# A table of powers on one partition, heads innermost, read in pieces of 4 KB

## The chip, the cores and the metric

The program runs on one core of a Trainium2 chip. What is measured is the time of one execution on the device, in microseconds (us). The core has a matrix engine (PE, TensorE), a vector engine (DVE), a scalar engine (ACT), a general engine (POOL), a queue engine that issues most transfers (SP), and 16 DMA engines that move data between HBM and the on-chip memory (SBUF). Matrix products are written to PSUM.

## The reference

Attention with a decay per head, block by block, followed by two gated layers. Cut to what matters here:

```
pos = arange(64);  rel = pos[:, None] - pos[None, :]
Dmask     = where(rel >= 0, lam ** rel, 0)            # per head, 8 heads
lam_pow   = lam ** (pos + 1);  lam_block = lam ** 64
rev_pow   = lam ** (63 - pos)
for each block b of 64 rows:
    intra = (q_b k_b^T * Dmask) v_b
    inter = (q_b * lam_pow) kv_state
    out_b = intra + inter
    kv_state = lam_block * kv_state + (k_b * rev_pow)^T v_b
x = out as (1536 tokens, 512)
h = x w_in;  g = h * tanh(softplus(h));  x = g w_out
h = x w2_in; g = max(h, 0)^2;            result = g w2_out
```

`q`, `k`, `v` are (2, 8, 768, 64), `lam` has 8 values between 0.97 and 0.99, `w_in` and `w2_in` are (512, 2048), `w_out` and `w2_out` (2048, 512). All is fp32.

## The kernel before

The kernel takes chunks of 128 rows in place of the blocks of 64: twelve chunks, six for each of the two batches, taken in pairs by `attention(j)`. The eight heads are four pairs (index `p` or `n`) times two (index `e`). For every chunk it loads `qk` and `kv` (512 KB each), makes the scores `sc` on PE (L392), multiplies them by the mask into `a` on DVE (the operation of L395, recorded as L271), weights `k` by the mask's last column on POOL (`kd`, L398) and `q` by the decays on POOL (`qd`, L403, not for the first chunk of a batch), makes the state's increment `sd` on PE (L415), scales the state by lam to the 128 (L451 on ACT in the first pairs, L447 on POOL later) and adds the increment on DVE (tile `state`). The output `xo` sums products of `a` with `v` (L433) and of the weighted `q` with the state (L437). It is split into a high and a low part (`xh` on ACT, `xl` on DVE) for the layers, whose products are `up`, `p`, `b`, `e` and `dn` (all recorded as L278). The weights arrive as 64-bit numbers in tiles `st`, from which `m` (ACT, L507), `t` (DVE, L510 and L515), `wh` (ACT) and `wl` (DVE) are made.

The mask and the decays come from one table of powers of `lam`. It lies on eight partitions, one for each head, as 256 columns: 127 zeros, a one, and lam to the 1 to 128 (`tab`, L300). `lam` is loaded into it by a transfer from ACT's queue (L334), `ones` writes the zeros and the one (L331, L332), `powers` doubles the number of filled columns seven times (L324). The table is written to HBM (`tab_d`, L338) and then read back so that partition j gets the table shifted by j: for the mask two transfers (L344), one for each `e`, whose innermost runs are 128 elements of one head (512 bytes), and for the decays two more (L351), the same runs repeated over 64 partitions each. In SBUF the mask is laid out as (e, pair, column), like the scores.

All operations are given to a planner with an estimated duration each. It fills the engines by due times and writes down one order, and every engine works through its instructions in that order. `FIRST` (L241) fixes the order of the first transfers on SP's queue: st00000, qk0, tab_d, kv0, st00001, masks, decays, qk1, kv1, qk2, kv2, qk3, kv3. Every instruction waits for the data it needs, and those behind it on its engine wait with it. On-chip tiles of 4 KB per partition are handed out by the planner (`UNITS` of them) and given back after the last use. A number behind a name counts chunks (`a0` is the first `a`, `qk5` the sixth `qk`).

Of the kernel before, what the change touches and what calls it, by code (L numbers as in the profile page):

```python
# [12 lines left out]
F32 = mybir.dt.float32  # L13
# [7 lines left out]
P = 128  # L21
# [195 lines left out]
def attention_mlps(ctx, tc, lam, qk, kv, w_in, w_out, w2_in, w2_out, out):  # L217
# [52 lines left out]
    def tt(o, a, b, alu):  # L270
        nc.vector.tensor_tensor(out=o, in0=a, in1=b, op=alu)  # L271
# [19 lines left out]

    W = 2 * CH
    tab_d = dram.tile([H, W], F32, name="tab_d")
    misc = Val("misc")
    mask = Val("mask")

    def pw():
        return tl(misc, 2, 4, CH)[:, 0]

    def tab():  # L300
        return tl(misc, 4, W)[0:H, 2]

# [8 lines left out]
    misc_parts = [(misc, "pw"), (misc, "tab")]  # L311
# [9 lines left out]
    def powers():  # L321
        t, o, n = tab(), CH - 1, 1
        while n < CH:
            nc.vector.tensor_scalar(  # L324
                out=t[:, o + n + 1 : o + 2 * n + 1], in0=t[:, o + 1 : o + n + 1],
                scalar1=t[:, o + n : o + n + 1], scalar2=None, op0=ALU.mult,
            )
            n *= 2

    def ones():  # L330
        nc.vector.memset(tab()[:, 0 : CH - 1], 0.0)  # L331
        nc.vector.memset(tab()[:, CH - 1 : CH], 1.0)  # L332

    op("ACT", 0.1, lambda: nc.scalar.dma_start(out=tab()[:, CH : CH + 1], in_=lam), [], [(misc, "lam")],  # L334
       name="lam", lag=2.2, due=0.0)
    op("DVE", 0.4, ones, [], [(misc, "tab")], name="ones")
    op("DVE", 1.2, powers, [(misc, "lam")], [(misc, "tab")], name="powers")
    op("SP", 0.1, lambda: nc.sync.dma_start(out=tab_d, in_=tab()), [(misc, "tab")], [("tab_d", 0)],  # L338
       name="tab_d", lag=2.2, due=FIRST["tab_d"])

    def masks():
        for e in range(2):

            nc.sync.dma_start(  # L344
                out=tl(mask, 2, NP, CH)[:, e],
                in_=bass.AP(tab_d.tensor, tab_d.offset + e * W, [[1, P], [2 * W, NP], [1, CH]]),
            )

    def decays():
        for e in range(2):  # L350
            nc.sync.dma_start(  # L351
                out=pw()[e * D : (e + 1) * D],
                in_=bass.AP(tab_d.tensor, tab_d.offset + e * W + CH, [[0, D], [2 * W, NP], [1, CH]]),
            )

    op("SP", 1.6, masks, [("tab_d", 0)], [(mask, 0)], name="masks", due=FIRST["masks"])
# [526 lines left out]
```

## Time and profile before

| what | us |
|---|---|
| median of 3 runs | 566.46 (566.30 to 566.48) |
| the profiled execution | 566.5 |
| its span, from first to last instruction | 564.7 |
| PE busy | 549.6 (97%) |
| PEld (weight loads, beside PE) busy | 454.9 |
| ACT busy | 333.2 |
| DVE busy | 307.6 |
| POOL busy | 33.1 |

The page gives the busy time of each engine, the span in 40 slices, and the chain of work that ended last. A timeline lists instructions in order of time: start, duration (of all merged instructions together), engine, line, operation, output<-inputs, shapes, count, and in brackets how long the engine had been idle before and what ended that. An engine's name with a small q (SPq) is its queue, where transfers are issued. All times count from the span's start.

### The profile page before, as it was taken

Reading aid. Unit: us, or ns where it says so; the run is one execution under the profiler, and the core shown is the slowest. Engines: PE = TensorE matmul, PEld = TensorE weight load, DVE = VectorE, ACT = ScalarE, POOL = GpSimd, SP = SyncE. Lnnn points to the kernel's source line nnn. Section 1 sums busy time; section 2 is a strip of 40 time slices with the busy share of each in tenths; the row PEclk is TensorE's granted clock in tenths of the full one; section 3 lists DMA queues with packets and bytes.
Section 4 is the critical chain, followed back from the end, with each engine's and each line's share of the span. In section 5 each row is a group of like instructions: output and inputs, shape, how many; then the busy total and the mean of one; then the engine's idle time right before and its main releaser. Section 6 shows DMA issues by size and latency. Waiting matters only on the chain.

```text
span 564.7 us, 7047 instructions
## 1 busy us (share of the span) xinstructions
PE 549.6 (97%) x2934; PEld 454.9 (81%) x2934; DVE 307.6 (54%) x339; ACT 333.2 (59%) x374; POOL 33.1 (6%) x31
## 2 busy tenths in 40 slices
PE   3989999999999999999999999999999999999997
PEld 1878888888888888888888888888888888888885
DVE  2876985951453833582688865434363635743301
ACT  1435364643764566545886877347964789546920
POOL 1654600000000000000000000000000000000000
PEclk9899999999999999999999999999999999999999
DMA  8999000222141106041400401311222112300022
GB/s 238 409 409 339 6 2 0 75 74 74 38 149 38 38 2 203 21 122 65 149 1 0 150 0 38 111 39 37 76 74 75 60 48 79 113 0 1 18 95 111
DMA packets 15998, 50.52 MB, mean 89 GB/s; under 512 B 1624, under 2 KB 3168, under 8 KB 15968
## 3 DMA queue, kind: packets, MB, share of 16 engines
q1 hardware_dynamic: 15952, 50.08, 25.5%
q8 instruction: 23, 0.38, 0.3%
q14 instruction: 7, 0.06, 0.0%
q10 hardware_dynamic: 16, 0.00, 0.0%
HBM read 46.92 MB, written 3.15 MB: 89 GB/s over the span
## 4 chain that ended last, share of the span: by engine, by line
PE 96%; DMA 2%; DVE 1%; issue 0%; SPq 0%; DVEq 0%
PE dn L278 46%; PE up L278 20%; PE p L278 13%; PE e L278 7%; PE b L278 3%; PE xo L433 2%; PE sc L392 2%; PE xo L437 1%; DMA mask<-tab_d 1%; PE sd L415 1%; DVE t L510 0%; DMA tab_d<-misc 0%; DVE state L271 0%; DVE misc L324 0%; DMA misc<-in_lam_dram 0%
## 5 line engine op out<-in xcount | busy, mean ns | idle before, releaser
L515 DVE SCALAR_TENSOR_TENSOR t<-m,t 128x1024 int32<-128x1024 int32 x64 | 78.5, 1231 | 63.5 <-ACT m L507 61.4
L268 ACT ACTIVATE ac<-dn 128x1024 f32<-128x1024 f32 x46 | 47.3, 1029 | 101.9 <-PE dn L278 101.9
L271 DVE TENSOR_TENSOR gl<-h,gh 128x1024 fp32r<-128x1024 f32 x48 | 58.7, 1227 | 78.0 <-ACT gh L268 77.6
L278 PE MATMUL dn<-gh,wl 128*128 128x512 f32 x192 | 74.7, 389 | 0.0
L278 PE MATMUL dn<-wh,gh 128*128 128x512 f32 x192 | 74.7, 389 | 0.0
L278 PE MATMUL dn<-wh,gl 128*128 128x512 f32 x192 | 74.7, 389 | 0.0
L278 PE MATMUL dn<-gh,wh 128*128 128x512 f32 x192 | 74.7, 389 | 0.0
L278 PE MATMUL dn<-wl,gh 128*128 128x512 f32 x192 | 74.7, 389 | 0.0
L278 PE MATMUL dn<-gl,wh 128*128 128x512 f32 x192 | 74.7, 389 | 0.0
L268 ACT ACTIVATE gh<-h 128x1024 fp32r<-128x1024 f32 x48 | 50.3, 1053 | 0.7
L507 ACT ACTIVATE m<-st 128x512 f32<-128x512 f32 x64 | 40.1, 664 | 10.5 <-DMA st<-in_moe_w_in_dram 6.8
L271 DVE TENSOR_TENSOR wl<-t,wh 128x1024 fp32r<-128x1024 f32 x32 | 39.6, 1246 | 12.1 <-ACT wh L268 12.1
L606 ACT ACTIVATE h<-up 128x1024 f32<-128x1024 f32 x20 | 20.6, 1029 | 38.2 <-PE up L278 32.5
L268 ACT ACTIVATE wh<-t 128x1024 fp32r<-128x1024 f32 x32 | 33.4, 1052 | 15.3 <-DVE t L515 15.2
L278 PEld LDWEIGHTS dn<-gh,wl 128*128 128x128 f32 x192 | 36.0, 188 | 7.5
L278 PEld LDWEIGHTS dn<-wh,gh 128*128 128x128 f32 x192 | 36.0, 188 | 7.5
L278 PEld LDWEIGHTS dn<-gl,wh 128*128 128x128 f32 x192 | 36.0, 188 | 7.5
L278 PEld LDWEIGHTS dn<-wl,gh 128*128 128x128 f32 x192 | 36.0, 188 | 7.5
L278 PEld LDWEIGHTS dn<-wh,gl 128*128 128x128 f32 x192 | 36.0, 188 | 7.4
L278 PEld LDWEIGHTS dn<-gh,wh 128*128 128x128 f32 x192 | 36.0, 188 | 7.4
L268 ACT ACTIVATE dn<-ac 128x1024 f32<-128x1024 f32 x34 | 34.4, 1019 | 0.2
L510 DVE TENSOR_SCALAR t<-st 128x512 int32<-128x512 int32 x64 | 26.8, 446 | 7.0 <-DMA st<-in_moe_w_in_dram 5.7
(102 smaller groups left out, 987.3 us busy)
## 6 DMA issues: line engine op xcount, KB each, us to landing
st<-in_moe_w_in_dram SPq DMA_DIRECT2D x32, 512.0 KB, 4.7
st<-in_moe_w_out_dram SPq DMA_DIRECT2D x32, 512.0 KB, 3.6
qk<-in_qk_dram SPq DMA_DIRECT2D x12, 512.0 KB, 10.6
kv<-in_kv_dram SPq DMA_DIRECT2D x12, 512.0 KB, 10.4
out_dram<-ac SPq DMA_DIRECT2D x4, 512.0 KB, 2.8
out_dram<-ac SPq DMA_DIRECT2D x4, 256.0 KB, 2.0
mask<-tab_d SPq DMA_DIRECT2D x2, 256.0 KB, 6.3
misc<-tab_d SPq DMA_DIRECT2D x2, 128.0 KB, 6.8
```

What stands on the lines that cost most here:

```text
L268: nc.scalar.activation(out=o, in_=i, func=AF.Copy)
L271: nc.vector.tensor_tensor(out=o, in0=a, in1=b, op=alu)
L278: nc.tensor.matmul(out=out_, lhsT=a, rhs=b, start=first and i == 0 and not onto, stop=last and i == 2, skip_group_check=onto)
L392: nc.tensor.matmul(out=o[:, e, p], lhsT=t[r, 1, p], rhs=t[r, 0, p], start=True, stop=True)
L415: nc.tensor.matmul(out=o[e * D : (e + 1) * D, p], lhsT=t[:, p, 1 + e], rhs=t[:, p, 0 if e else 3], start=True, stop=True)
L433: nc.tensor.matmul(out=o[e * D : (e + 1) * D, p, n], lhsT=v[:, p, 0 if e else 3], rhs=w[:, e, p], start=True, stop=fresh)
L437: nc.tensor.matmul(out=o[r, p, n], lhsT=z[:, p, r], rhs=qd[:, p], start=False, stop=True)
L507: op("ACT", 0.67, lambda st=st, i=i: nc.scalar.activation(out=tl(m)[:, i], in_=tl(st, TB, 2)[:, :, 1].bitcast(F32), func=AF.Copy, scale=RA ...
L510: op("DVE", 0.5, lambda st=st, i=i: nc.vector.tensor_scalar(out=tl(t)[:, i], in0=tl(st, TB, 2)[:, :, 0], scalar1=29, scalar2=None, op0=ALU ...
L515: nc.vector.scalar_tensor_tensor(out=tl(t), in0=tl(m).bitcast(I32), scalar=scalar, in1=tl(t), op0=shift, op1=ALU.bitwise_or)
L606: op("ACT", 1.05, lambda: nc.scalar.activation(out=tl(h), in_=tl(src), func=AF.Relu if L else AF.Mish), halves(src), [(h, 0)], name=h.name)
```

## The change

The table now lies on one partition in two tiles of 4 KB, with the eight heads innermost: element (column, head). `ones` and `powers` work on whole rows of eight heads, `powers` with a product of two operands, the second repeated. `lam` is loaded as one row of eight. The table is written to HBM by two transfers, one for each tile. The mask is read by one transfer whose rows are 4 KB long, each starting eight elements after the one before; the decays by two transfers whose rows are 4 KB less one element. In SBUF mask and decays keep the order (column, head), so `a` (through `weighting`) and `qd` (through `pw`) read them with a step of eight elements. The planner's estimates for `powers`, `masks` and `decays` change from 1.2, 1.6 and 0.9 to 2.0, 0.8 and 0.6 us.

```diff
     W = 2 * CH
-    tab_d = dram.tile([H, W], F32, name="tab_d")
+    tab_d = dram.tile([1, W * H], F32, name="tab_d")
     misc = Val("misc")
+    table = [Val("tab0"), Val("tab1")]
     mask = Val("mask")
     def pw():
-        return tl(misc, 2, 4, CH)[:, 0]
-    def tab():
-        return tl(misc, 4, W)[0:H, 2]
+        return tl(misc, CH, NP, 2)[:, :, :, 0].rearrange("p i n -> p n i")
+    def weighting():
+        return tl(mask, CH, NP, 2).rearrange("p i n e -> p e n i")
+    def tab(lo, hi):
+        t, b = table[lo // CH], lo // CH * CH
+        return tl(t, CH, H)[0:1, lo - b : hi - b]
     def warm_up():
@@ -308,7 +315,6 @@
     warm = Val("warm", "P")
     zval = Val("zero", dtype=BF16)
-    misc_parts = [(misc, "pw"), (misc, "tab")]
     def zeros():
         if zval.tile is None:
@@ -319,42 +325,46 @@
     op("PE", 4.3, warm_up, [(zval, 0)], [(warm, 0)], name="warm", rank=-3000)
     def powers():
-        t, o, n = tab(), CH - 1, 1
+        o, n = CH - 1, 1
         while n < CH:
-            nc.vector.tensor_scalar(
-                out=t[:, o + n + 1 : o + 2 * n + 1], in0=t[:, o + 1 : o + n + 1],
-                scalar1=t[:, o + n : o + n + 1], scalar2=None, op0=ALU.mult,
-            )
+            nc.vector.tensor_tensor(
+                out=tab(CH + n, min(CH + 2 * n, W)), in0=tab(CH, min(CH + n, W)),
+                in1=tab(CH + n - 1, CH + n).to_broadcast([1, n, H]), op=ALU.mult)
             n *= 2
     def ones():
-        nc.vector.memset(tab()[:, 0 : CH - 1], 0.0)
-        nc.vector.memset(tab()[:, CH - 1 : CH], 1.0)
-    op("ACT", 0.1, lambda: nc.scalar.dma_start(out=tab()[:, CH : CH + 1], in_=lam), [], [(misc, "lam")],
-       name="lam", lag=2.2, due=0.0)
-    op("DVE", 0.4, ones, [], [(misc, "tab")], name="ones")
-    op("DVE", 1.2, powers, [(misc, "lam")], [(misc, "tab")], name="powers")
-    op("SP", 0.1, lambda: nc.sync.dma_start(out=tab_d, in_=tab()), [(misc, "tab")], [("tab_d", 0)],
-       name="tab_d", lag=2.2, due=FIRST["tab_d"])
+        nc.vector.memset(tab(0, CH - 1), 0.0)
+        nc.vector.memset(tab(CH - 1, CH), 1.0)
+    op("ACT", 0.1, lambda: nc.scalar.dma_start(out=tab(CH, CH + 1), in_=lam.rearrange("(o h) w -> w o h", o=1)),
+       [], [(table[1], 0)], name="lam", lag=2.2, due=0.0)
+    op("DVE", 0.4, ones, [], [(table[0], 0)], name="ones")
+    op("DVE", 2.0, powers, [(table[1], 0)], [(table[1], 0)], name="powers")
+    def write():
+        for i in range(2):
+            nc.sync.dma_start(out=tab_d[:, i * CH * H : (i + 1) * CH * H], in_=tl(table[i], 1, CH * H)[0:1, 0])
+    op("SP", 0.1, write, [(v, 0) for v in table], [("tab_d", 0)], name="tab_d", lag=2.2, due=FIRST["tab_d"])
     def masks():
-        for e in range(2):
-            nc.sync.dma_start(
-                out=tl(mask, 2, NP, CH)[:, e],
-                in_=bass.AP(tab_d.tensor, tab_d.offset + e * W, [[1, P], [2 * W, NP], [1, CH]]),
-            )
+        nc.sync.dma_start(
+            out=tl(mask, 1, CH * H)[:, 0],
+            in_=bass.AP(tab_d.tensor, tab_d.offset, [[H, P], [1, CH * H]]),
+        )
     def decays():
         for e in range(2):
             nc.sync.dma_start(
-                out=pw()[e * D : (e + 1) * D],
-                in_=bass.AP(tab_d.tensor, tab_d.offset + e * W + CH, [[0, D], [2 * W, NP], [1, CH]]),
+                out=tl(misc, 1, CH * H)[e * D : (e + 1) * D, 0, 0 : CH * H - 1],
+                in_=bass.AP(tab_d.tensor, tab_d.offset + CH * H + e, [[0, D], [1, CH * H - 1]]),
             )
-    op("SP", 1.6, masks, [("tab_d", 0)], [(mask, 0)], name="masks", due=FIRST["masks"])
-    op("SP", 0.9, decays, [("tab_d", 0)], [(misc, "pw")], name="decays", due=FIRST["decays"])
+    op("SP", 0.8, masks, [("tab_d", 0)], [(mask, 0)], name="masks", due=FIRST["masks"])
+    op("SP", 0.6, decays, [("tab_d", 0)], [(misc, "pw")], name="decays", due=FIRST["decays"])
     x_hi, x_lo, x_raw = {}, {}, {}
@@ -392,12 +402,12 @@
                         nc.tensor.matmul(out=o[:, e, p], lhsT=t[r, 1, p], rhs=t[r, 0, p], start=True, stop=True)
             op("PE", 0.95, scores, [(q, "q"), (q, "k")], [(sc, 0)], name=sc.name, rank=rank + n)
-            op("DVE", 1.3, lambda a=a, sc=sc: tt(tl(a, 2, NP, CH), tl(sc, 2, NP, CH), tl(mask, 2, NP, CH), ALU.mult),
+            op("DVE", 1.3, lambda a=a, sc=sc: tt(tl(a, 2, NP, CH), tl(sc, 2, NP, CH), weighting(), ALU.mult),
                [(sc, 0), (mask, 0)], [(a, 0)], name=a.name)
             if not (last and n):
                 op("POOL", 1.3, lambda k=k: nc.gpsimd.tensor_tensor(
                     out=tl(k, NP, 4, D)[:, :, 1:3], in0=tl(k, NP, 4, D)[:, :, 1:3],
-                    in1=tl(mask, 2, NP, CH)[:, :, :, CH - 1 : CH].rearrange("p e n o -> p n e o").to_broadcast(
+                    in1=tl(mask, CH, NP, 2)[:, CH - 1].rearrange("p n (e o) -> p n e o", o=1).to_broadcast(
                         [P, NP, 2, D]), op=ALU.mult), [(k, "k"), (mask, 0)], [(k, "k")], name=f"kd{c}")
             if not first or n:
                 op("POOL", 1.35, lambda q=q: nc.gpsimd.tensor_tensor(
```

## Rows read from the trace of the kernel before

**Rows 1.** The page: busy time of engines, share of span, instructions.
```profile
PE 549.6 (97%) x2934; PEld 454.9 (81%) x2934; DVE 307.6 (54%) x339; ACT 333.2 (59%) x374; POOL 33.1 (6%) x31
```

**Rows 2.** Stages: window, length, busy us of engines (instructions), PEclk, DMA, GB/s.
```profile
0.00:14.30 14.30, 5.12 (x26) 2.26 (x26) 4.08 (x14) 2.62 (x3) 2.39 (x7) 0.90 0.85 240
14.30:33.00 18.70, 16.75 (x258) 14.80 (x258) 16.05 (x21) 8.22 (x19) 10.60 (x10) 0.90 1.03 408
33.00:66.00 33.00, 32.73 (x445) 28.48 (x446) 23.63 (x28) 13.97 (x18) 19.07 (x16) 1.00 0.69 264
66.00:558.00 492.00, 492.00 (x2200) 407.21 (x2195) 262.49 (x278) 308.42 (x334) 1.02 (x1) 1.00 0.18 61
```

**Rows 3.** Waits of PE: engine, line, awaited, total us, times, longest.
```profile
PE xo L433 <- DVE a L271: 6.8, 1, 6.8
```

**Rows 4.** The chain that ended last: start us, us, what.
```profile
3.92 1.78 DMA tab_d<-misc
...
6.15 6.75 DMA mask<-tab_d
```

**Rows 5.** Timeline of DVE, the head.
```profile
0.86 0.27 DVE L318 MEMSET zero<- 128x256 uint32 x1 [0.86 <-PEq L870]
1.09 0.16 DVE L331 MEMSET misc<- 8x127 f32 x1
...
2.13 1.76 DVE L324 TENSOR_SCALAR misc<-misc 8x1 f32<-8x1 f32 x7 [0.87 <-DMA misc<-in_lam_dram]
...
10.06 0.43 DVE L510 TENSOR_SCALAR t<-st 128x512 int32<-128x512 int32 x1 [4.52 <-DMA st<-in_moe_w_in_dram]
```

**Rows 6.** Timeline of DVE, 18 to 63 us.
```profile
18.34 1.23 DVE L271 TENSOR_TENSOR a<-sc,mask 128x1024 f32<-128x1024 f32 x1 [1.70 <-PE sc L392]
...
26.85 0.88 DVE L271 TENSOR_TENSOR state<-sd,state 64x256 f32<-64x256 f32 x2 [0.39 <-PE sd L415]
27.76 2.33 DVE L510 TENSOR_SCALAR t<-st 128x512 int32<-128x512 int32 x2
...
32.33 0.69 DVE L271 TENSOR_TENSOR xl<-xo,xh 128x512 fp32r<-128x512 f32 x1
...
62.74 0.87 DVE L271 TENSOR_TENSOR state<-sd,state 64x256 f32<-64x256 f32 x2 [0.94 <-POOL state L447]
```

**Rows 7.** Timeline of SP's queue, 4 to 6 us.
```profile
4.72 0.42 SPq L502 DMA_DIRECT2D st<-in_moe_w_in_dram  x1
5.72 0.94 SPq L344 DMA_DIRECT2D mask<-tab_d  x2
```

**Rows 8.** Transfers, 8.5 to 13.5 us: packets by size.
```profile
DMA packets 1698, 1.16 MB, mean 231 GB/s; under 512 B 77, under 2 KB 1607, under 8 KB 1698
```

**Rows 9.** Stages, two stretches of the head.
```profile
5.00:6.00 1.00, 0.15 (x1) 0.00 (x0) 0.43 (x1) 0.67 (x1) 0.00 (x0) 1.00 0.82 242
8.50:13.50 5.00, 0.00 (x0) 0.00 (x0) 0.90 (x2) 0.67 (x1) 0.43 (x1) 0.78 1.05 231
```

**Rows 10.** Groups of POOL by shape: count, busy us, mean ns, idle before.
```profile
L403 POOL TENSOR_TENSOR qk<-qk,misc 128x512 f32<-128x512 f32 x10 | 12.9, 1300 | 7.1 <-PE sc L392 7.1
L398 POOL TENSOR_TENSOR kv<-kv,mask 128x512 f32<-128x512 f32 x10 | 10.9, 1092 | 18.6 <-DMA mask<-tab_d 11.4 <-DMA kv<-in_kv_dram 7.2
```

**Rows 11.** Timeline of POOL.
```profile
27.32 1.06 POOL L398 TENSOR_TENSOR kv<-kv,mask 128x512 f32<-128x512 f32 x1 [1.97 <-DMA kv<-in_kv_dram]
...
56.98 3.74 POOL L403 TENSOR_TENSOR qk<-qk,misc 128x512 f32<-128x512 f32 x3
```

**Rows 12.** Timeline of PE.
```profile
28.09 0.39 PE L437 MATMUL xo<-qk,state 128*64 128x128 f32 x4
...
31.13 1.16 PE L392 MATMUL sc<-qk 64*128 64x128 f32 x16 [1.33 <-DMA qk<-in_qk_dram]
...
33.08 0.50 PE L278 MATMUL up<-xl,wh 128*128 128x512 f32 x1
...
64.64 0.39 PE L437 MATMUL xo<-qk,state 128*64 128x128 f32 x4
```

## The prediction, made before the kernel was run

> **What bounds the kernel now.** The first view is the page. The span is 564.7 us and TensorE is busy for 549.6 us of it, 97% [rows 1]; the profiled execution took 566.5 us, 1.8 us more than its span, and the median of the three runs shown is 566.46 us, so a shift of the span can be added to the median as it is. The change removes no TensorE work. It can therefore win or lose only where TensorE is idle, which is 15.1 us in all. The stages [rows 2] say where: 9.2 us before 14.3 us, 2.0 us from there to 33 us, 0.3 us to 66 us, nothing from 66 to 558 us, and about 3.7 us at the end, which the change does not touch. The waits of TensorE [rows 3] name the largest: 6.8 us, in one piece, for the first `a` (scores times mask). So all that matters lies ahead of 33 us, with a possible echo up to 66 us.
>
> The chain of waits [rows 4] shows the 6.8 us as a relay: `lam` lands at 2.1 us, seven table steps end at 3.9 us, the table's write lands 1.8 us later, the mask is issued at 5.72 us and lands 6.75 us after the second of its transfers is issued, and then DVE makes `a`. The change touches every leg of that relay.
>
> **Part by part: the table.** `ones` now sets 127 x 8 = 1016 columns on one partition in place of 127 columns on eight. The rows for 127 and 256 columns take 164 and 272 ns [rows 5], a slope of 0.84 ns, so I estimate 0.9 us; it would begin at 1.09 us as now and end just about when `lam` lands (2.11 us). It is hidden, with no cover left; every tenth above that is on the path. `powers` keeps seven dependent steps, 0.25 us from start to start, 1.76 us in all. They now cover 1016 columns instead of 127, and each is a two-source product. A two-source product takes 1.23 us for 1024 columns and 0.69 us for 512 [rows 6], so 1.05 ns for each. Charged on top of the old chain that is +1.07 us; with the fixed part of the wider form (0.69 - 512 x 1.05 ns = 0.15 us a step) it is +0.75 us. I take +0.9 us.
>
> The table's write is now two transfers of 4 KB from one partition each. The first needs only `ones` and leaves early; the second leaves at 4.8 in place of 3.92 us. It is not seen how a transfer from one partition lands; I keep the 1.8 us, with 0.3 us either way. On SP's queue kv0 and st00001 stand between this write and the mask; the second is seen in [rows 7], so these two, 1 MB, also leave 0.9 us later, and so does the mask: 6.6 in place of 5.72 us. Of the two places where DMA issues change in number, the table gains one and the mask loses one, so whatever is queued after the mask keeps its place.
>
> **The mask's transfer.** From 8.5 to 13.5 us nearly all packets are below 2 KB (1607 of 1698 [rows 8]), and 231 GB/s are moved although the DMA engines are busy throughout [rows 9]; in the stretch after it 408 GB/s are moved [rows 2]. Five microseconds at 231 GB/s are 1.16 MB, which would take 2.8 us at 408, so pieces of 4 KB can save at most 2.2 us. Not all of the loss need be the small packets: from 5 to 6 us, where large packets follow large ones, 242 GB/s are moved [rows 9], some 0.4 us lost without any small packet. The other end is no saving at all, or a little loss, if reading one 8 KB table from all sides is what is slow. I check the middle by landings: st00001 lands at 10.06 us [rows 5]; 0.9 us later that is 11.0 us, and 512 KB behind it at 408 GB/s take 1.3 us. The mask then lands at about 12.2 in place of 12.9 us: -0.7, and I take -0.8 us, because the mask no longer shares its stretch with short `decays` packets. The loads behind (qk1 and on) gain about the same. So much of what the pieces win, some 1.7 us, is spent on the late start.
>
> **The step of eight.** Every `a` now reads its mask with a step of eight elements, 32 bytes. No row of before shows such a read. Below, it may be free: the row of `t<-st` reads 512 columns with a step of two in 0.43 us where it runs undisturbed [rows 5], no dearer per column than a packed product (1.23 us for 1024). Above: a step of eight spreads the elements four times as far as that row does, and if each read then takes two slots in place of one, the streamed part of an `a` doubles, 1024 x 1.05 ns = +1.07 us. Neither end has a near row, so I take +0.6 us for each of the twelve, about the middle, and keep both ends.
>
> [...]
>
> On POOL, `qd` reads the decays with the same step. Reading a whole second operand instead of a repeated element makes 1.30 out of 1.09 us [rows 10]; I take +0.3 us for the step, with nothing and a doubling (+1.3 us) as ends.
>
> **What of it is on the path.** `a0` is: +0.6 against -0.8 us, so xo0 starts 0.2 us earlier. From 18.34 us on DVE works through `a1`, `a2`, `a3` and their fellows with hardly more than one idle piece of 0.39 us to 33.0 us [rows 6]. So it reaches the state update of 26.85 us at 26.46 - 0.8 + 4 x 0.6 = 28.1 us, 1.2 us late. TensorE needs that update for xo3, whose state products start at 28.09 us [rows 12]; their slack is 0.36 us, so xo3 ends 0.85 us late. This costs nothing yet, since TensorE then idles 1.33 us for qk5 [rows 12], which lands earlier by 0.8 us. What counts is the last `xl` (32.33 + 0.69 = 33.02 us), for the third `up` product starts at 33.08 us right behind it [rows 6, 12]. Before it stand the two `t` of 27.76 us, which took 2.33 us where two such take 0.86 us undisturbed; POOL was at work on `kd4` from 27.32 us, and on `qd4` behind it [rows 11]. POOL starts from the landing of kv4, earlier by 0.8 us, DVE comes 1.2 us later, so part of that overlap goes; I take half, -0.7 us. The sum at `up` is -0.8 + 2.4 - 0.4 - 0.7 = +0.5 us.
>
> Beyond it `a4` and `a5` run at 37.55 us for products at 44 us. From 55.83 us three `a` stand before the state update of 62.74 us: +1.8 us against 0.94 us of idle time on DVE and then 1.03 us until xo10 reads the state at 64.64 us [rows 6, 12]; the three `qd` there add 0.9 us on POOL beside it [rows 11]. At my prices this is covered; beyond +0.66 us for an `a` it costs three times the excess. From 66 to 558 us TensorE is never idle, so what is lost by then stays lost. Sum: 566.46 + 0.5 = 567.0 us.
>
> **The rivals.** *A, faster: the step of eight is free.* The step of two speaks for it [rows 5]. Then the head follows the mask alone: with the saving between mine and the upper bound, the mask is 0.8 to 1.8 us earlier, `xl` likewise, since qk5 comes earlier too. Time: 566.46 - 1.3 = 565.2 us.
> *B, slower: DVE, working in order, becomes the bound.* The place is the row of work from `a1` to the last `xl`, which has 0.39 us of slack; the price is four times the extra of an `a` at 33 us and three times the excess over 0.66 us at 64 us. It passes +0.2% from about +0.72 us on. At +1.07 us it is 4.3 - 0.8 - 0.4 - 0.7 = 2.4 us, and 1.2 us at xo10: 570.0 us. [...] Against it: `a` takes its other operand from PSUM, which the rows of packed reads do not price apart.
> *C: the change does not do what it says.* All rows of the mask come out of one 8 KB table; if that, and not the size of the pieces, held the stretch to 231 GB/s, only the delay of 0.9 us stays. Then +0.9 + 2.4 - 0.4 - 0.7 = +2.2 us: 568.7 us. Against it: 512-byte rows fill the whole of the slow stretch and end with it.
>
> **How the numbers follow.** My forecast, 567.0 us with 566.0 to 567.6 us as its own range, gets 0.42; A 0.20, B 0.26, C 0.12. Below 565.3 us is faster by over 0.2%, above 567.6 us slower; about 0.2% is what a measurement of this kernel can tell from no change. So faster 0.20, same 0.42, slower 0.38. The range of 8 in 10 leaves out the far half of A and the dearest of B: 565.1 to 569.8 us.
>
> **What would show it.** The rows of `a` give the price of the step at once (1.23 us now; 1.8 by my sum, 2.3 by B); `qd` likewise (1.30 us). The mask's landing should be near 12.2 us, its issue near 6.6 us, and the stretch behind st00001 should move over 300 GB/s; below 250 is C. xo3's state products should wait for DVE, and `xl` end near 33.5 us. The prediction is wrong if `a` stays at 1.23 us, if the table's write from one partition takes over 2.5 us to land, or if TensorE finds a new wait after 66 us.

## The result, and the profile after

The changed kernel takes 572.57 us (median of 4, 572.31 to 572.97) against 566.47 us before: a ratio of 1.0109, 95% interval 1.0091 to 1.0126, so 6.1 us slower, above the predicted range. Its profiled execution took 572.31 us with a span of 570.2 us, 2.1 us outside the span where before had 1.8. All ratios here leave out two executions that ran in a far slower state, one of a test kernel below, g1 (621.8 us), and one of the kernel before (1435 us).

The page (as [rows 1]) and the stages of the kernel after (as [rows 2]):

```profile
PE 552.1 (97%) x2934; PEld 456.5 (80%) x2934; DVE 318.7 (56%) x339; ACT 333.0 (58%) x374; POOL 38.6 (7%) x31
```

```profile
0.00:14.30 14.30, 5.61 (x26) 2.32 (x26) 5.69 (x13) 2.64 (x3) 2.76 (x7) 0.81 0.83 238
14.30:33.00 18.70, 15.74 (x248) 14.24 (x250) 16.45 (x18) 8.13 (x19) 11.48 (x9) 0.87 1.02 407
33.00:66.00 33.00, 30.35 (x366) 25.52 (x364) 25.73 (x26) 12.73 (x16) 19.05 (x13) 0.95 0.71 273
66.00:558.00 492.00, 491.90 (x2270) 407.77 (x2267) 268.04 (x281) 309.48 (x336) 5.29 (x4) 1.00 0.18 60
```

TensorE's instructions are as many as before, but it is busy 2.5 us longer and idle 3.0 us longer. After 66 us nothing moves. New against [rows 2] is the stretch from 33 to 66 us: 30.35 us busy in place of 32.73, at a granted clock of 0.95 in place of 1.00. The waits of TensorE after (as [rows 3]) name the new one, the second line:

```profile
PE xo L443 <- DVE a L271: 7.3, 1, 7.3
PE up L278 <- DVE xl L271: 2.3, 1, 2.3
PE sc L402 <- DMA qk<-in_qk_dram: 2.1, 2, 1.5
```

DVE's timeline shows what made `xl` late: first four lines of before that [rows 6] leaves out, then after.

```profile
22.64 1.37 DVE L271 TENSOR_TENSOR wl<-t,wh 128x1024 fp32r<-128x1024 f32 x1
24.04 0.69 DVE L271 TENSOR_TENSOR xl<-xo,xh 128x512 fp32r<-128x512 f32 x1
...
30.19 1.23 DVE L515 SCALAR_TENSOR_TENSOR t<-m,t 128x1024 int32<-128x1024 int32 x1
31.44 0.86 DVE L271 TENSOR_TENSOR state<-sd,state 64x256 f32<-64x256 f32 x2
```

```profile
18.74 2.04 DVE L271 TENSOR_TENSOR a<-sc,mask 128x1024 f32<-128x1024 f32 x1 [1.70 <-PE sc L402]
...
25.39 2.08 DVE L271 TENSOR_TENSOR a<-sc,mask 128x1024 f32<-128x1024 f32 x1
27.39 0.68 DVE L271 TENSOR_TENSOR xl<-xo,xh 128x512 fp32r<-128x512 f32 x1
28.08 0.88 DVE L271 TENSOR_TENSOR state<-sd,state 64x256 f32<-64x256 f32 x2
28.99 1.85 DVE L271 TENSOR_TENSOR wl<-t,wh 128x1024 fp32r<-128x1024 f32 x1
30.76 1.74 DVE L520 TENSOR_SCALAR t<-st 128x512 int32<-128x512 int32 x1
32.53 0.88 DVE L271 TENSOR_TENSOR state<-sd,state 64x256 f32<-64x256 f32 x2
33.43 0.43 DVE L520 TENSOR_SCALAR t<-st 128x512 int32<-128x512 int32 x1
33.90 1.95 DVE L525 SCALAR_TENSOR_TENSOR t<-m,t 128x1024 int32<-128x1024 int32 x1
35.88 0.69 DVE L271 TENSOR_TENSOR xl<-xo,xh 128x512 fp32r<-128x512 f32 x1
```

The groups of all twelve `a`, before and after (count, busy us, mean ns, idle before):

```profile
L271 DVE TENSOR_TENSOR a<-sc,mask 128x1024 f32<-128x1024 f32 x12 | 14.6, 1221 | 8.7 <-PE sc L392 5.9 <-DMA mask<-tab_d 2.5
L271 DVE TENSOR_TENSOR a<-sc,mask 128x1024 f32<-128x1024 f32 x12 | 25.2, 2109 | 8.9 <-PE sc L402 6.8 <-DMA mask<-tab_d 2.0
```

Two things are to be seen. Each of these `a` takes 2.0 to 2.1 us in place of 1.23. And the order is another one: `wl` stood ahead of the first `xl` before, and now stands behind the state update of 28.08 us; the second state update stands between the two `t`. The diff moves none of these. The planner did, because three of its estimates changed.

POOL's groups (as [rows 10]), and the `kd` and `qd` that run beside that `wl` and the first `t`:

```profile
L413 POOL TENSOR_TENSOR qk<-qk,misc 128x512 f32<-128x512 f32 x10 | 16.8, 1687 | 10.8 <-PE sc L402 10.8
L408 POOL TENSOR_TENSOR kv<-kv,mask 128x512 f32<-128x512 f32 x10 | 12.8, 1288 | 17.0 <-DMA mask<-tab_d 11.0 <-DMA kv<-in_kv_dram 6.0
```

```profile
28.71 1.04 POOL L408 TENSOR_TENSOR kv<-kv,mask 128x512 f32<-128x512 f32 x1 [1.85 <-DMA kv<-in_kv_dram]
29.71 2.50 POOL L413 TENSOR_TENSOR qk<-qk,misc 128x512 f32<-128x512 f32 x1
```

The next two fences are TensorE's timelines, first of before and then of after: the scores that stand behind the `up` products, and the last product of all; for after also the scores that wait and the third `up` (as [rows 12]).

```profile
41.05 1.16 PE L392 MATMUL sc<-qk 64*128 64x128 f32 x16
...
560.62 0.39 PE L278 MATMUL dn<-wh,gh 128*128 128x512 f32 x1
```

```profile
32.53 1.16 PE L402 MATMUL sc<-qk 64*128 64x128 f32 x16 [1.51 <-DMA qk<-in_qk_dram]
...
36.62 0.80 PE L278 MATMUL up<-xl,wh 128*128 128x512 f32 x1 [2.27 <-DVE xl L271]
...
45.99 1.16 PE L402 MATMUL sc<-qk 64*128 64x128 f32 x16
...
566.06 0.39 PE L278 MATMUL dn<-wh,gh 128*128 128x512 f32 x1
```

| place | before | after | late by |
|---|---|---|---|
| third `up` product starts | 33.08 | 36.62 | 3.54 |
| scores behind the `up` products | 41.05 | 45.99 | 4.94 |
| last product | 560.62 | 566.06 | 5.44 |
| profiled execution | 566.5 | 572.31 | 5.8 |

From the third `up` to the scores the same products took 9.37 us in place of 7.97. Two windows of the kernel after (columns as in [rows 2]) show why:

```profile
34.00:36.00 2.00, 0.35 (x2) 0.00 (x0) 1.97 (x2) 0.00 (x0) 1.55 (x2) 1.00 1.01 406
36.00:38.00 2.00, 1.38 (x3) 1.16 (x4) 2.00 (x3) 0.14 (x1) 2.00 (x2) 0.56 1.04 414
```

TensorE stood nearly still from 34 to 36 us (0.35 us busy), and in the following 2 us the granted clock was 0.56; from 38 to 40 us it was 0.59, and from 40 us it is 1.00 again.

So the 5.8 us of the profile are 3.5 us of a late `xl`, 1.4 us of clock, 0.5 us in small pieces behind, and 0.3 us outside the span (with rounding).

The head, by the chain of waits after (as [rows 4]) and the stretch of [rows 9]:

```profile
3.72 0.69 DVE tab L331
4.41 0.02 issue
4.43 1.44 DMA tab_d<-tab
...
5.93 6.62 DMA mask<-tab_d
```

```profile
8.50:13.50 5.00, 0.00 (x0) 0.00 (x0) 1.27 (x2) 0.68 (x1) 0.81 (x1) 0.54 1.00 266
```

The table ends 0.5 us later than before, its write lands sooner (1.44 us), the mask is issued only 0.2 us later and lands at 12.55 in place of 12.90 us. The stretch moves 266 GB/s in place of 231. The landing alone is not clear of the spread between traces: with before's table and its transfers on SP's queue the first `a` starts at 12.3 to 13.0 us in seven traces, with the new table and whole decays at 11.9 to 12.7 us in nine.

### The profile page after: what moved, and what is told of

It reads as the page before. It is cut to its first block, busy times and chain, and to the rows that moved or that the text cites. A ratio compares the mean times of both kernels' runs of the same rounds, so it can differ in the third digit from the quotient of the medians.

```text
span 570.2 us, 7054 instructions
## 1 busy us (share of the span) xinstructions
PE 552.1 (97%) x2934; PEld 456.5 (80%) x2934; DVE 318.7 (56%) x339; ACT 333.0 (58%) x374; POOL 38.6 (7%) x31
## 4 chain that ended last, share of the span: by engine, by line
PE 91%; DVE 4%; DMA 1%; issue 1%; POOL 1%; ACT 0%; DVEq 0%; POOLq 0%; SPq 0%
PE dn L278 46%; PE up L278 19%; PE p L278 13%; PE e L278 7%; PE b L278 3%; DVE a L271 2%; PE xo L443 1%; DMA mask<-tab_d 1%; PE xo L447 1%; PE sc L402 1%; DVE state L271 1%; DVE t L520 0%; DVE tab L331 0%; DVE xl L271 0%; POOL state L457 0%
## 5 line engine op out<-in xcount | busy, mean ns | idle before, releaser
L525 DVE SCALAR_TENSOR_TENSOR t<-m,t 128x1024 int32<-128x1024 int32 x64 | 78.9, 1237 | 63.0 <-ACT m L517 61.4
L271 DVE TENSOR_TENSOR a<-sc,mask 128x1024 f32<-128x1024 f32 x12 | 25.2, 2109 | 8.9 <-PE sc L402 6.8
```

Of the source, the lines that this page charges most:

```text
L525: nc.vector.scalar_tensor_tensor(out=tl(t), in0=tl(m).bitcast(I32), scalar=scalar, in1=tl(t), op0=shift, op1=ALU.bitwise_or)
```

## The experiments

**The step of eight alone, the order alone, and both.** Kernel before with only the operand of `a` changed; kernel before with only the three estimates changed; kernel before with both.

```diff
-tt(tl(a, 2, NP, CH), tl(sc, 2, NP, CH), tl(mask, 2, NP, CH), ALU.mult)
+tt(tl(a, 2, NP, CH), tl(sc, 2, NP, CH), tl(mask, CH, NP, 2).rearrange("p i n e -> p e n i"), ALU.mult)
```

```diff
-    op("DVE", 1.2, powers, ...   op("SP", 1.6, masks, ...   op("SP", 0.9, decays, ...
+    op("DVE", 2.0, powers, ...   op("SP", 0.8, masks, ...   op("SP", 0.6, decays, ...
```

> The kernel before, with its table, its transfers and its order, but the products a read the mask with a step of eight (the weights are then in the wrong order, so the result differs). Theory S: each a takes 2.0 to 2.2 us and the time rises to 570 to 571.5 us by DVE's row of work ahead of the first up products alone: 4 x 0.9 - 0.4 = 3.2 us there, 1 us at 64 us. Theories L and O: below 568 us, since neither the loads nor the order have moved.

> The kernel before with the three planner estimates of the changed kernel (powers 2.0, masks 0.8, decays 0.6 us) and nothing else: the instructions are the same, DVE has them in the changed kernel's order ahead of 40 us (one wl after the state update instead of before an xl). Theory S and L: within 0.6 us of the kernel before, 566 to 567 us. Theory O: 568 us or more.

> The kernel before, its table and its transfers, with both the step of eight in a (weights in the wrong order, so the result differs) and the changed kernel's order on DVE. Theory SO (they add up): 566.5 + 1.8 + 1.7 = 570 us. If they add more than that, TensorE's clock is the reason: the granted clock after 33 us falls below 1.0 as in the changed kernel, and the time is 571 us or more. If the order has nothing to lose once the a are long: 568.5 to 569 us.

Measured: the step 568.49 us, ratio 1.0027 (1.0017 to 1.0038); the order 568.44 us, 1.0034 (1.0017 to 1.0050); both 570.84 us, 1.0072 (1.0049 to 1.0094). In e3 the first four `a` take 2.00 to 2.07 us each and the third `up` starts at 34.80 us, 1.7 us late. e3 met neither mark: the step is a cost, but only about half of what was expected of it alone. e5 met theory O. Either alone costs about a quarter to a third of the loss, and together they cost about their sum (0.72% against 0.61%). e7 is still 1.7 us below the kernel after; how much of that is clock is taken up below.

**The kernel after with one of the two undone.** Packed reads in `a` (e1), in `a` and `qd` (e2), and the kernel after with before's three estimates (e6):

```diff
     def pw():
-        return tl(misc, CH, NP, 2)[:, :, :, 0].rearrange("p i n -> p n i")
+        return tl(misc, 2, 4, CH)[:, 0]
     def weighting():
-        return tl(mask, CH, NP, 2).rearrange("p i n e -> p e n i")
+        return tl(mask, 2, NP, CH)
```

> The changed kernel, but the products a read the mask packed, without the step of eight; the weights are then in the wrong order, so the result differs, while each instruction keeps its size. Theory S (the step of eight on DVE is the cost; an a took 2.11 us after against 1.22 us before): the rows of a return to 1.22 us and most of the 6.1 us goes; 567 to 568 us, what is left being the later loads (qk5 landed 1.4 us later after the change). Theory L (the later table and loads are the cost): the a become shorter but the time stays above 570 us. Theory O (the planner's other order on DVE is the cost): as L, above 569.5 us.

> As e1_a_packed, and POOL's qd read the decays packed too (wrong order again, same sizes). Theory S: qd returns from 1.69 to 1.30 us; if POOL's step matters by itself, 0.5 us or more below e1_a_packed; if it is covered, within 0.4 us of it. Theory L: equal to e1_a_packed and above 570 us.

> The changed kernel with the planner estimates of the kernel before, so with DVE's order of before (wl ahead of the xl instead of after the state update). Theory SO (the step of eight and the order on DVE add up, each being worth 1.7 us by itself on the kernel before): about 2 us below the changed kernel, 570 to 571 us. Theory S alone (the step does it, the order costs only where DVE has gaps to lose, and with long a it has none): within 0.7 us of the changed kernel, 572 us.

Measured: e1 568.94 us, 1.0033 (1.0019 to 1.0048); e2 568.19 us, 1.0028 (1.0015 to 1.0041); e6 568.78 us, 1.0038 (1.0024 to 1.0052). So e2, which has the table and the new order but no step, is about where the order alone is (e5), and e6, which has table and steps but the old order, about where the step alone is (e3). The table itself does not show in these medians, nor does POOL's step (e2 against e1: the intervals of the ratios overlap for the most part). Two marks were missed: e1 lies above theory S's 568 us and below what the others asked, and e6 lies below both of its theories, so that the order, with the clock that goes with it, is worth more in the kernel after than alone. DVE's timeline of e6, to be held against that of after:

```profile
24.47 1.23 DVE L271 TENSOR_TENSOR wl<-t,wh 128x1024 fp32r<-128x1024 f32 x1
...
29.80 2.10 DVE L520 TENSOR_SCALAR t<-st 128x512 int32<-128x512 int32 x2
32.00 1.22 DVE L525 SCALAR_TENSOR_TENSOR t<-m,t 128x1024 int32<-128x1024 int32 x1
33.25 0.86 DVE L271 TENSOR_TENSOR state<-sd,state 64x256 f32<-64x256 f32 x2
34.14 0.69 DVE L271 TENSOR_TENSOR xl<-xo,xh 128x512 fp32r<-128x512 f32 x1
```

In the old order `wl` ran at 24.5 us in 1.23 us and the last of these operations (L525) in 1.22 us; in the kernel after the same two fall beside POOL's `kd` and `qd` and its state scaling and take 1.85 and 1.95 us. `xl` starts at 34.14 in place of 35.88 us. The long `wl` does not come from the order alone: e5, e7 and h2 have it at the same place, in 1.23 us. In e7, whose `kv` lands 0.7 us earlier (`kd` starts behind it at 28.03 in place of 28.71 us), `wl` stood ahead of POOL's `qd`, and it is the `qd` that is longer:

```profile
29.00 1.23 DVE L271 TENSOR_TENSOR wl<-t,wh 128x1024 fp32r<-128x1024 f32 x1
```

```profile
29.23 2.13 POOL L403 TENSOR_TENSOR qk<-qk,misc 128x512 f32<-128x512 f32 x1
```

**Which of the order's moves.** Kernel before, with a planner line that moves only `wl` behind the second state update (h1), or `wl` behind the first and the second state update ahead of the second `t`, as in after (h2). Where the two texts say that a3 is moved or passed, the state update of that chunk is meant.

```diff
+    plan.follow(named["sa3"], named["wl0000"])     # h1
+    plan.follow(named["sa2"], named["wl0000"])     # h2
```

> The kernel before with one thing changed: DVE's order ahead of 40 us is that of the kernel after (wl behind the state update that follows a2, a3 ahead of the second t); all estimates, later orders, transfers and operands are before's. Theory that the early moves carry the cost of the order: as long as before with the three new estimates, 568.2 to 568.6 us (ratio 1.003), xl ending near 33.5 us, wl no longer than 1.3 us, third up near 33.6 us. Rival, that the cost lies in the few orders changed after 40 us or in the time outside the span: 566.6 to 567.0 us and an xl that ends by 33.2 us.

> The kernel before with only wl moved, behind a3, ahead of which it stood; nothing else is moved. If moving wl out of the idle time of DVE ahead of 26 us is what costs, then DVE idles there as in the kernel with the new estimates (about 0.9 us twice) and the last xl comes 0.5 to 1.0 us later: 567.4 to 568.6 us. If it is a3 being ahead of the second t that costs, this one is within 0.1% of before.

Measured: h2 568.36 us, 1.0027 (1.0014 to 1.0041), `xl` at 33.61 us (32.33 before), third `up` at 34.36 us; h1 567.01 us, 1.0004 (0.9987 to 1.0022), `xl` at 32.19 us, though DVE idles 0.95 and 0.88 us ahead of it as in the kernel with the new estimates. So the first theory for h1 falls by its trace (by time alone its interval still reaches into the expected range), and `wl` may stand in the late stretch at no cost that is seen; h2 met its mark in time, though its `xl` ended and its third `up` started 0.8 us later than expected. The same operations stand ahead of `xl` in both. In h1 the pair of `t` and L515 took 0.76 and 1.89 us and the whole piece from 26.29 us to `xl` 5.9 us; in h2 `t`, `t` and L515 took 1.28, 0.47 and 1.95 us and the piece from 26.85 us 6.8 us. The `t` of h1, then the first of h2:

```profile
27.19 0.76 DVE L510 TENSOR_SCALAR t<-st 128x512 int32<-128x512 int32 x2
```

```profile
28.90 1.28 DVE L510 TENSOR_SCALAR t<-st 128x512 int32<-128x512 int32 x1
```

It is not how much stands ahead of `xl`, then, but where it falls beside POOL's work; that this is the mechanism is read from the lengths, and was not tried by itself. The rest of the 1.4 us between the two `xl` is the head, which was 0.56 us later in h2. h2 carries most of what the estimates cost in e5 (0.27 of 0.34%).

**The clock.** The kernel after once more; then with the scores of the sixth chunk, behind the `up` products, made three times (e8); then with those of the seventh, which stand at the start of the wait, made three times (e9). Nothing else is changed; e9 fills part of the idle time and adds 1.8 us of work to it.

```diff
-            def scores(sc=sc, q=q):
+            def scores(sc=sc, q=q, times=3 if c == 6 else 1):   # e9; e8: c == 5
...
-                for p in range(NP):
+                for p in [p for _ in range(times) for p in range(NP)]:
```

> The changed kernel once more, beside the next three on one chip. All theories: 572 to 573 us, with the third up product near 36.6 us and TensorE's granted clock below 0.6 from 36 to 40 us.

> The changed kernel with the scores of the sixth chunk made three times over (the same result each time), 2.2 us more work for TensorE just where it waits for the last xl, from 33.6 us on. Theory C (TensorE's idle time from 31 to 36.6 us made its granted clock fall, which costs 1.3 us in the up products that follow): the granted clock stays at 1.0 from 36 to 40 us and the time falls by 1 to 1.5 us in spite of the added work, to 571 to 571.5 us. Without theory C: 572.5 us or more.

> The changed kernel with the scores that TensorE makes at 32.6 us (the seventh chunk's) made three times over, the same result each time: 2.2 us of work just where TensorE waits 2.3 us for the last xl. (In e8_scores_thrice the repeated scores were those at 44 us, behind the up products, not in the wait.) Theory C (the idle time ahead of 36.6 us lets the granted clock fall to half, which costs 1.3 us): the granted clock stays at 1.0 from 36 to 40 us and the time falls by 1 to 1.5 us, to 571 to 571.5 us. Without theory C: 572.3 us or more, the clock falling all the same.

Measured: again 572.53 us, 1.0095 (1.0073 to 1.0117), clock 0.60 from 36 to 38 us; e8 572.41 us, 1.0108 (1.0081 to 1.0134); e9 570.79 us, 1.0073 (1.0053 to 1.0093), 1.7 us below the kernel after with more work, though the intervals of the two ratios overlap. e8 does not test what its text says: its repeated scores ran from 44.4 us, behind the wait. Of e9:

```profile
32.09 2.95 PE L402 MATMUL sc<-qk 64*128 64x128 f32 x48 [1.46 <-DMA qk<-in_qk_dram]
...
36.18 0.50 PE L278 MATMUL up<-xl,wh 128*128 128x512 f32 x1 [0.47 <-DVE xl L271]
...
44.12 1.16 PE L402 MATMUL sc<-qk 64*128 64x128 f32 x16
```

```profile
36.00:38.00 2.00, 1.82 (x8) 1.52 (x9) 1.98 (x3) 0.58 (x1) 2.00 (x2) 1.00 1.02 406
```

`xl` is only 0.45 us earlier than in after, but the `up` products take 7.94 us instead of 9.37: the clock is worth 1.4 us. It does not fall every time: in e8 with a wait of 2.26 us, and in e7 with one of 2.11 us, it stayed at 1.00 and the `up` products took 7.93 and 7.97 us, so the 1.8 us that e8 adds behind are hidden in its total by the dip that it did not have. The repeated run of after has one execution with a mean clock of 0.993, whose span is 568.4 us beside 570.1 to 570.3 us for the three at 0.984 to 0.988; but one execution of the first run had 0.997 and 570.4 us, without a trace. So the dip is shown to cost 1.4 us where it comes; when it comes is open, and so is whether the filled wait kept it away in e9, since e8 kept the full clock with the wait unfilled.

The kernel before has executions of a lower clock too. Of its 102 executions beside these experiments 29 have a mean clock of 0.987 and take 568.24 us in the median; the other 73 take 566.58 us. No trace of one of the 29 is on record, so where their clock fell is not seen. Every median therefore carries how many such executions it caught: none of the four of before beside the first result, by their times, but six of the eight of after (0.984 to 0.988). Set against the executions of before above 0.987 that ran beside them, those above 0.988 are longer by 1.9 us with the step (e3), 1.7 us with the order (e5), 3.5 us with both (e7, two executions) and 4.3 us in the kernel after (one). By this split step and order add up, about 0.8 us is left for the table and POOL's step together, and the remaining 1.8 us of the 6.1 us are the clock. It was made after the fact, rests on few executions, and the one of after at 0.997 (572.97 us) does not fit it.

**The table and its transfers alone.** The kernel after with packed reads in `a` and `qd` and before's estimates, so that only the table, its write and the longer pieces are new (e10):

> The changed kernel with the order of before on DVE and with a and qd reading packed (weights in the wrong order, so the result differs): what is left of the change is the table on one partition and its transfers of 4 KB. If pieces of 4 KB win what the prediction said: 565.3 to 565.8 us, the mask landing near 12.2 us. If they win nothing (the mask landed at 12.5 in place of 12.9 us in the changed kernel, and the loads behind it came no earlier): 566.0 to 567.0 us.

Measured: 567.32 us, 1.0004 (0.9992 to 1.0016), above both marks. None of its ten executions has the mean clock of 0.987; six of the nineteen of before beside them have, and the other thirteen take 566.65 us, so the table may cost 0.7 us that the ratio hides. The mask lands at 12.6 us, but the scores that wait for `qk` start at 32.21 us, 1.1 us later than before (31.13 us [rows 12]). Two kernels move the mask. In d1 it is read from 128 different rows of `qk`; in f1 the kernel before issues it from ACT's queue:

```diff
-            in_=bass.AP(tab_d.tensor, tab_d.offset, [[H, P], [1, CH * H]]),
+            in_=qk[NCHUNK - 1],                    # d1, on e10
-            nc.sync.dma_start(
+            nc.scalar.dma_start(                   # f1, on before, masks()
```

> As e10_table_alone, but the mask's 128 rows of 4 KB are read from 128 places of an input (the last qk) and not from the one 8 KB table (so the mask holds other numbers); its issue no longer waits for the table, so it leaves some 0.4 us earlier. Theory T (many reads of the same 8 KB of HBM are slow): the stretch from 8.5 to 13.5 us moves over 330 GB/s in place of about 265, and the mask lands 1 us or more earlier, below 11.5 us. Theory H (the decays, written to one half of the partitions at a time, or the start of new transfers are slow): the rate stays below 300 GB/s and the mask lands at 11.8 to 12.3 us.

> The kernel before, with the two transfers of the mask issued from ACT's queue in place of SP's, so that they need not stand behind kv0 and st00001; all orders else as before. The mask should land near 10 us in place of 12.9. Theory that the loads of qk are the next bound: the scores still wait for qk until about 31 us, and the time is 566.0 to 566.8 us, no gain that counts. Rival, that the whole relay ahead of the first a is on the path: 2 us faster or more, below 565 us.

Measured: d1 566.74 us, 0.9997 (0.9986 to 1.0008), mask at 11.6 us, 317 GB/s from 8.5 to 13.5 us, and TensorE waits 5.7 us for the first `a` and then 2.5 us for `qk`. It lies between its two theories, and its mask also left 0.3 us earlier (5.58 us); from issue to landing it took 6.0 us, where the shared table took 6.7 us in e10 and, by estimate, 5.9 us in e2 (landing at 11.8 us, the issue taken at 5.9 us as in after, e10 and d2). So one trace of d1 does not show that the shared table is slow. f1 missed its aim: the mask landed at 14.3 us, not 10, since ACT's queue issued it at the same time as SP did before (5.65 against 5.72 us), and SP issued the decays beside it at 5.65 and qk1 at 7.04 us; and yet 567.19 us, 1.0002 (0.9990 to 1.0015). TensorE waits 8.2 us for the first `a` and then 0.7 us for `qk`. One microsecond early or one and a half late, the mask alone moves nothing that these intervals show (0.9986 to 1.0015): what it gives, the wait for `qk` takes back. What counts more is when the loads are through.

**The bytes of the decays.** Transfers until 33 us, before and then e10: issues of the decays, KB each, median us to landing.

```profile
misc<-tab_d SPq DMA_DIRECT2D x2, 128.0 KB, 6.8
```

```profile
misc<-tab_d SPq DMA_DIRECT2D x2, 255.8 KB, 7.9
```

A row of 4 KB carries all eight heads where a partition needs four, so the decays move 512 KB in place of 256. g1 is e10 with rows cut to 2 KB (256 KB in all); g2 is the kernel before with its two transfers issued twice; d2 is e10 with both decays in one transfer of 128 partitions.

```diff
-                in_=bass.AP(tab_d.tensor, tab_d.offset + CH * H + e, [[0, D], [1, CH * H - 1]]),
+                in_=bass.AP(tab_d.tensor, tab_d.offset + CH * H + e, [[0, D], [1, CH * H // 2]]),   # g1
-        for e in range(2):
+        for e in (0, 1, 0, 1):                                                                     # g2
+            in_=bass.AP(tab_d.tensor, tab_d.offset + CH * H, [[1, 2], [0, D], [1, CH * H - 1]]),    # d2
```

> The kernel after with before's estimates and order, with mask and decays read packed (so the numbers are out of place: left out is the order of columns and heads), and with the two decays transfers cut to rows of 2 KB, 128 KB each as before, where after moves 255.8 KB each. Theory that the doubled decays ate the gain of the 4 KB pieces: the seventh chunk's scores, which wait for qk, start near 31.5 us in place of 32.2 us (0.26 MB less at 408 GB/s is 0.64 us), and the time is 0.1% below before, 566.4 us or less against 567.0 for the same kernel with the full decays. Rival, that the loads are late for another reason: no move, scores at 32.1 us or later.

> The kernel before with the two decays transfers issued twice, the same bytes to the same place: 256 KB more on SP's queue ahead of qk1, in runs of 512 bytes. By the theory the scores that wait for qk start 0.6 to 1.1 us later than before's 31.13 us (256 KB at 408 and at 231 GB/s) and the time grows by 0.1 to 0.2%. Rival, that the loads have slack: no move, within 0.05%.

> As e10_table_alone, but the decays come in one transfer to all 128 partitions in place of two transfers to 64 each (same bytes, same rows). Theory H: the stretch from 10.5 to 14.5 us moves 330 GB/s or more in place of about 265, qk1 and the loads behind it land 0.5 to 1 us earlier. Theory T: below 300 GB/s as before, no change of the loads over 0.3 us.

g1: 566.46 us, 0.9986 (0.9975 to 0.9996), the only kernel whose interval lies below 1. That need not be a gain: none of g1's executions has the mean clock of 0.987, five of before's seventeen have, and the other twelve take 566.54 us. TensorE's line of e10 and then of g1:

```profile
32.21 1.16 PE L402 MATMUL sc<-qk 64*128 64x128 f32 x16 [1.66 <-DMA qk<-in_qk_dram]
```

```profile
31.56 1.16 PE L402 MATMUL sc<-qk 64*128 64x128 f32 x16 [1.79 <-DMA qk<-in_qk_dram]
```

The scores start 0.65 us earlier, as 0.26 MB at 408 GB/s would have it, and outside the 32.05 to 32.63 us of the eight other traces (d2 aside) with whole decays and a shared table. It is one trace, and the bytes need not be all: in d1, with whole decays and the mask from its own rows, they start at 31.35 us. The mask lands at 11.7 us, but e2 with whole decays has it at 11.8. It is not a version to use, since its numbers are out of place.

g2 says little about bytes: 570.22 us, 1.0054 (1.0040 to 1.0068), but the second pair waited 4.5 us on SP's queue for the first, which writes the same place, and the loads behind waited with it. From this one reads only that this stall of the load queue, 4.5 us long, cost 3.3 us.

d2: 579.76 us, 1.0228 (1.0206 to 1.0250), which neither theory has. Its wait of TensorE:

```profile
PE sc L400 <- DMA qk<-in_qk_dram: 14.1, 3, 12.7
```

From 14.3 to 33 us only 227 GB/s are moved, where e10 moves 408. Why one transfer in place of two comes to this is not shown: the run has only the sum of all engines.

## Why the prediction was wrong

The step that failed is the sum at `up`. It shifts DVE's row of work as a whole, with its order as before, and has no term for another order nor for the clock. Put the measured 0.89 us for an `a` into the prediction's own sum and it gives 4 x 0.89 - 0.8 - 0.4 - 0.7 = 1.7 us at `up` and 0.7 us at xo10, 568.8 us, inside the stated range; and e6, the kernel after in before's order, measured 568.78 us, with its third `up` 1.8 us late. That they agree this closely is in part luck, since the mask and the relief were both taken too large. What the runs showed in place of the missing term is 3.8 us more from the new order, the dip of the clock included.

Up to the start of `xl` the two timelines of DVE add up, 35.88 - 32.33 = 3.55 us: mask -0.35, four `a` +3.31 (8.20 against 4.89 us), `wl` +0.48, L525 +0.72, `t` -0.16, and -0.45 us of idle time and rounding. Step by step:

- *What bounds the kernel*: the place held. After 66 us nothing moved, and all but 0.5 us came from ahead of 46 us. That the change could lose only where TensorE is idle did not hold: of 5.5 us more span 2.5 us are busy time, 1.4 us of it by the lower clock.
- *The `a`*: that the step costs was right, the size was not: +0.89 us in the mean of twelve (2109 against 1221 ns), not +0.6; four of them 3.3 instead of 2.4 us. The middle was taken between ends that no row bore out, and the upper end was nearer. The rows show 2.0 us and more for a step of eight elements, 32 bytes, with the other operand in PSUM. The step of two, 0.43 us for 512 columns [rows 5], did not tell of a step of eight.
- *The relief of 0.7 us beside POOL*: failed in the new order. The two `t` took 2.17 us in place of 2.33, and `wl` and L525 came to lie beside POOL's work. In before's order it came in part: 1.79 us in e3, 2.10 us in e6. POOL's `qd` was longer as forecast: 1.54 to 1.57 us where nothing disturbed it, +0.27 where +0.3 was taken (mean of all 1687 instead of 1300 ns).
- *The order, which was taken as unchanged*: the term that was missing. Alone it costs 1.5 to 1.9 us (h2, e5), and undoing it in the kernel after gives 3.8 us back (572.5 to 568.8 us, e6), dip of the clock included. The diff's three estimates were named ahead of the prediction and then given no line in the sum.
- *The clock*: missing too, 1.4 us in the profiled execution; there it came behind the idle piece that the late `xl` makes. It stayed away with that piece filled (e9), but also with it unfilled (e8), and before has executions of a lower mean clock too, so its cause stays open.
- *The mask*: issue expected at 6.6, seen at 5.93 us, since the write landed in 1.44 us in place of 1.8 and the table cost 0.5 us in place of 0.9 (the prediction's own terms, seven steps of 0.15 us and 1.07 us against 1.76 us, come to +0.36, not to the +0.75 written there); landing expected at 12.2, seen at 12.55 us. The gain of the pieces was over-counted, 0.35 us instead of 0.8, and no run shows it to be worth anything (e10, d1, f1). "The loads behind gain about the same" failed: the scores behind them start at 32.05 us or later where the shared table and the whole decays are read, at 31.13 us before, and 0.65 us of that go with half of the decays' bytes (g1).
- *`ones`*: 0.91 us against 0.9; it started 0.2 us later than the row before it suggested, and its end still met the landing of `lam`.
- *The rivals*: B named the right engine and place, but with 570.0 us at its dearest it lacked order and clock. C's mark was a stretch below 250 GB/s; it moved 266, or 317 with rows of its own for each partition (d1), which fits a shared table that holds it back in part but is one trace. A fell with the first `a`.
- *The signs of being wrong*: none of the three came (`a` at 1.23 us, a write over 2.5 us, a new wait after 66 us). They cover terms of the sum, and what was missing had no term.

Not settled: every kernel with the new estimates spends 2.0 to 2.6 us outside the span, every one with before's, h2 too, 1.7 to 1.9 us (of these d2 alone 2.0 to 2.1). For after that is 0.3 to 0.8 us of the loss, and no view shows it.

No version beat the kernel before and kept its numbers. The best is the kernel before, with its own order and packed reads.

## What to carry to other kernels

Where a planner writes the order, a changed estimate is a change of order: hold the two orders against each other first, and give every moved instruction its line in the sum. A layout that makes a transfer cheap once is paid at every read of it (here 0.89 us in each `a`), so price the twelve reads before the one transfer, and count the bytes as well as the size of the pieces. And before a transfer's gain is counted, ask what its consumer waits for next.

## What the runs showed of the hardware

- A product of two fp32 operands of 1024 columns, one from PSUM and one from SBUF with a step of eight, takes 2.00 to 2.25 us on DVE (the twelve `a` of after) against 1.21 to 1.23 packed (before).
- In the kernel after, operations of DVE beside POOL's were longer: `wl` 1.85 us (1.23 in e6), a `t` of 512 columns 1.74 (0.43 at 10.21 us), L525 1.95 (1.22 in e6). The `t` of 1.74 us ended at 32.50 us, the `qd` beside it at 32.21 us; where `wl` stood ahead (e7), it took 1.23 us and the `qd` 2.13 us. Why the one or the other is longer is not shown.
- The granted clock fell to 0.56 after a wait of 2.27 us in a busy stretch (after) and to 0.60 after the same wait in its repeat, not after one of 2.26 us (e8) or 2.11 us (e7), and cost 1.4 us. Of the kernel before 29 of 102 executions have a mean clock of 0.987, and they are 1.7 us longer in the median.
